# Second state sum moved ahead of the first gate product, and three weight requests reordered

## The chip, the cores and the metric

The kernel runs on one NeuronCore of a Trainium2 chip. The metric is the device time of one execution in microseconds (us); less is better. The engines named below are PE (TensorE, matrix products), DVE (VectorE), ACT (ScalarE), POOL (GpSimd) and SP (SyncE, which here only issues transfers). ACT issues transfers too.

## The reference

Two blocks follow one another, all in float32. First an mLSTM cell over batch 4, 8 heads, 768 steps, head size 40: for each step t it computes

```
m_new = max(f + m, i)
C = exp(f + m - m_new) * C + exp(i - m_new) * outer(v, k)
n = exp(f + m - m_new) * n + exp(i - m_new) * k
y = sigmoid(o) * (C q) / max(|n.q|, 1)
```

Then y is put together to 3072 tokens by 320 features, x, and a gated feed-forward block computes `(silu(x @ w_gate) * (x @ w_val)) @ w_out`, with 1536 hidden features.

The arrays reach the kernel in their own number format. The three weight matrices are 64-bit floats there: one weight is two 32-bit words, and the kernel makes a float32 of them.

## The kernel before, in words

**Tiles and groups.** The 768 steps are cut into six groups of 128 steps. The 32 heads of the batch are handled in two halves, called pairs P = 0 and P = 1, of 16 heads each. For a group the cell is computed with matrix products: scores inside the group, products with the state carried in, and an addition to the state. The result, x transposed (`xT`), is 320 features by 512 tokens (four batches of 128 steps).

**Feed-forward.** The 1536 hidden features are twelve chunks m of 128. `hidden(g, m)` (L643) does ten matrix instructions, which the trace records as 20 products of 512 columns (L648): they fill two PSUM banks, one for the gate and one for the value. ACT takes the Silu of the first (L653) and DVE multiplies it with the second into `h_sb` (L654). There are four banks of the kind "gen", so chunk m + 2 can begin only once ACT and DVE have read chunk m. `project` and `project_all` then multiply by `w_out`.

**The order of work.** Every engine's order is written out by hand: it is the order of the calls in the text. In group 0's feed-forward, lists named `ahead` and `slots` say what is done beside chunk m. In particular `slots[5]` and `slots[6]` hold the transposes of the next group's k and q, `slots[6]` and `slots[7]` the decay weights of the next group (`weights_sub` on DVE, L451, then `weights_mask` on POOL, L456), `slots[8]` their exponentials on ACT.

**Weights.** They come in pieces (`PIECES`, L138): pieces 0 and 1 hold one chunk each, pieces 2 to 6 two chunks each (piece 2: chunks 2 and 3, and so on), pieces 7 to 9 hold `w_out`. `piece_load` (L140) asks for a piece in two halves: the gate half goes to partitions 0 to 63, the value half to partitions 64 to 127. A half of pieces 2 to 6 is 640 KB. SP asks for the gate half. ACT asks for the value half of pieces 0 to 4, SP for those of pieces 5 and 6. A request waits in its engine's order like any other instruction, and the requests of one engine form one transfer queue.

A loaded chunk is made float32 by `convert`: `scale` (two passes on ACT, L190 and L192), `join` (two on DVE, L199 and L200) and `rounded` (L207, an addition on POOL, or on DVE where it is told so). Only then can PE multiply with it. Chunks 2 to 11 are converted inside the chunks before.

**The stretch around the change.** It is the end of the first group's cell, at 22 to 43 us. `sig` (L463) are the two sigmoids of the output gate on ACT. `first_own` and `first_x` make x, `first_gate` multiplies it with the sigmoid on DVE, `first_seam` transposes it to `xT`. Between the two seams stand six constant products, `burn(6, "gen")` (L469), on data that nothing reads. `first_state(P, eng)` (L547) sums the first group's state over its 128 steps with 16 matrix instructions for one pair (32 recorded, L552) and lets `eng` copy the sum to the state. `first_state(0, A)` runs before chunk 0, `first_state(1, A)` after it, in `slots[0]`. `slots[0]` also asks for the next group's k and q, which overwrite what the state sums read. The state is first needed by the next group, at 85 us.

SP's requests behind the weights are, in order: `M_sb` to `M_dram` (L611), k and q of the next group (L117), piece 6 (L165), `w_sb` from `M_dram` (L447, the next group's maxima), v, and so on.

Of the kernel before, what the change touches and what calls it, by code (L numbers as in the profile page):

```python
# [12 lines left out]
U32 = mybir.dt.uint32  # L13
# [11 lines left out]
def kernel(  # L25
# [18 lines left out]
    nc = tc.nc  # L44
# [7 lines left out]
    D1 = D + 1  # L52
# [4 lines left out]
    NKC = DM // HP  # L57
    UH = BH // 2
    UA = UH // 2
    NH = NFC + 1  # L60
# [15 lines left out]
    def bank(name, tag="cell"):  # L76
        return psum.tile([128, 512], F32, name=name, tag=tag)

    def half(i):
        return slice(i * SUB, (i + 1) * SUB)  # L80
# [5 lines left out]
    def heads(P):  # L86
        return slice(P * UH, (P + 1) * UH)

    k_sb = const.tile([128, BH, DP], F32)
    q_sb = const.tile([128, BH, DP], F32)  # L90
# [10 lines left out]
    wo_sb = const.tile([128, NFC, DM], F32)  # L101
    h_sb = const.tile([128, NH, TW], F32)
# [16 lines left out]
    def copy(eng, dst, src):  # L119
        if eng is nc.scalar:  # L120
            nc.scalar.copy(dst, src)
        else:
            eng.tensor_copy(dst, src)
# [13 lines left out]
    raws = {}  # L137
    PIECES = [("gv", 0, 1), ("gv", 1, 1)] + [("gv", m, 2) for m in range(2, NFC, 2)] + [("o", m, 4) for m in range(0, NFC, 4)]  # L138

    def piece_load(p, home=None):  # L140
        kind, m, n = PIECES[p]
        if kind == "gv":
            a, d = NKC, n * 128
            src = [(slice(i * HP, (i + 1) * HP), w[:, m * 128:(m + n) * 128].rearrange("(c p) f -> p c f", p=HP))
                   for i, w in enumerate((moe_w_gate, moe_w_val))]
            queues = (nc.sync, nc.scalar if p < 5 else nc.sync)
        else:
            a, d = n, DM
            src = [(slice(0, 128), moe_w_out[m * 128:(m + n) * 128].rearrange("(a p) d -> p a d", p=128))]
            queues = (nc.sync,)  # L150
        if src[0][1].dtype == F32:
            for r, w in src:
                if kind == "o":
                    nc.sync.dma_start(out=wo_sb[r, m:m + n, :], in_=w)
                else:
                    for x in range(n):
                        nc.sync.dma_start(out=wgv_sb[r, m + x], in_=w[:, :, ts(x, 128)])
            return
        if home is None:
            raw = conv.tile([128, 4 * NKC * 128], U32, name="raw")  # L160
        else:
            raw = home.rearrange("p a t -> p (a t)").bitcast(U32)
        raw = raw[:, 0:2 * a * d]
        for (r, w), queue in zip(src, queues):
            queue.dma_start(out=raw[r].rearrange("p (a d) -> p a d", a=a), in_=w.bitcast(U32))  # L165
        words = raw.rearrange("p (a d two) -> p a d two", two=2, a=a)
        raws[p] = (words[:, :, :, 0], words[:, :, :, 1])
        split(p)
# [4 lines left out]
    def split(p):  # L173
        if p in raws:
            lo, hi = raws.pop(p)
            kind, m, n = PIECES[p]
            if kind == "gv":
                for c in range(n):
                    r = slice(c * 128, (c + 1) * 128)
                    blocks[m + c] = (lo[:, :, r], hi[:, :, r], wgv_sb[:, m + c])  # L180
            else:
                for c in range(0, n, 2):
                    blocks[NFC + (m + c) // 2] = (lo[:, c:c + 2], hi[:, c:c + 2], wo_sb[:, m + c:m + c + 2, :])

    def scale(j):
        if j in blocks:
            lo, hi, dst = blocks[j]
            a, d = hi.shape[1], hi.shape[2]
            top = conv.tile([128, NKC * 128], F32, name="top", bufs=1).rearrange("p (a d) -> p a d", a=a)
            nc.scalar.mul(top, hi.bitcast(F32), 2.0 ** -112)  # L190
            low = conv.tile([128, NKC * 128], I32, name="low").rearrange("p (a d) -> p a d", a=a)
            nc.scalar.mul(low, lo, 2.0 ** -29)  # L192
            blocks[j] = (low, top.bitcast(U32), dst)

    def join(j):
        if j in blocks:
            lo, top, dst = blocks[j]
            both = dst.bitcast(U32)
            nc.vector.tensor_scalar(both, top, scalar1=3, scalar2=None, op0=ALU.logical_shift_left)  # L199
            nc.vector.scalar_tensor_tensor(both, in0=top, scalar=0x80000000, in1=both, op0=ALU.bitwise_and,  # L200
                                           op1=ALU.bitwise_or)
            blocks[j] = (lo, dst.bitcast(I32))

    def rounded(j, eng=None):
        if j in blocks:
            lo, dst = blocks.pop(j)
            (eng or nc.gpsimd).tensor_tensor(dst, dst, lo, op=ALU.add)  # L207

    def convert(j, eng=None):
        scale(j)  # L210
        join(j)
        rounded(j, eng)
# [34 lines left out]
    for u in range(B):  # L247
        r = slice(u * BH, (u + 1) * BH)
# [92 lines left out]
        eng.tensor_tensor(vw_sb[:, heads(P)], v_sb[:, heads(P)], w_sb[:, heads(P), last].to_broadcast([128, UH, D1]),  # L341
                          op=ALU.mult)

    def small(name, n=UA):
        return bank(name)[:, 0:n * D1].rearrange("p (a d) -> p a d", d=D1)

    def add(n, P):
        ps = [small("add") for _ in range(2)]
# [8 lines left out]
    def state(s):  # L357
        return C_ring[s % 3]
# [103 lines left out]
    def sig(P):  # L462
        nc.scalar.activation(o_sb[:, heads(P)], o_sb[:, heads(P)], AF.Sigmoid)  # L463


    def burn(n, tag="cell"):
        t = bank("burn", tag)
        for _ in range(n):
            nc.tensor.matmul(t, lhsT=junk[:, 0:128], rhs=junk, start=True, stop=True)  # L469
# [4 lines left out]
    A, V, G = nc.scalar, nc.vector, nc.gpsimd  # L474
# [66 lines left out]
    def first_gate(P):  # L541
        for u in (2 * P, 2 * P + 1):
            x = x_sb[:, u, 0:DM].rearrange("p (h d) -> p h d", d=D)
            nc.vector.tensor_tensor(x, x, o_sb[:, u * H:(u + 1) * H], op=ALU.mult)
        nc.gpsimd.tensor_copy(x_sb[:, 2 * P:2 * P + 2, DM:], x_sb[:, 2 * P:2 * P + 2, 0:HP])

    def first_state(P, eng):  # L547
        ps = small("add")
        for a in range(UA):
            for two in range(2):  # L550
                h = P * UH + 2 * a + two
                nc.tensor.matmul(ps[half(two), a, :], lhsT=k_sb[:, h, :], rhs=vw_sb[:, h, :], start=True, stop=True)  # L552
        copy(eng, state(2)[:, P * UA:(P + 1) * UA], ps)

    def first_seam(P, engs):
# [23 lines left out]
    first_turn(1, q_sb, qT, (A, V))  # L579
    load(o_sb, o_gate, 0, 1)  # L580
    piece_load(0)
    piece_load(1)
    late_maxima()
    first_own(1)
    first_values(1)
    first_scores(1)
    first_x(1)
    sig(0)
    sig(1)
    piece_load(2, h_sb[:, NH - NKC:])  # L590
    piece_load(3, wo_sb)
    burn(3)
    first_own(2)
    first_own(3)
# [3 lines left out]
    first_seam(0, (A, A, V))  # L598
    scale(0)
    first_gate(1)  # L600
    burn(6, "gen")
    piece_load(4)
    join(0)
    first_seam(1, (A, A, V))
    rounded(0, V)
    first_state(0, A)
    late_decay()
    convert(1)
    nc.scalar.activation(step1, step1, AF.Exp)
    piece_load(5)  # L610
    nc.sync.dma_start(out=M_dram, in_=flat(M_sb))  # L611
# [105 lines left out]
    def load_all(dst, a, n):  # L717
# [3 lines left out]
    run = lambda f, *a: (lambda: f(*a))  # L721
# [3 lines left out]
    ahead = {m: [m + 2] for m in range(4)}  # L725
    ahead.update({4: [6], 5: [7, 8], 6: [9], 7: [10], 8: [11], 9: [], 10: [], 11: []})
    slots = {
        0: [run(first_state, 1, A), run(load_all, k_sb, k, 1), run(load_all, q_sb, q, 1)],
        1: [run(piece_load, 6, h_sb[:, NH - NKC:]), run(decay_rows)],
        2: [run(late_turns), run(weights_load, 1), run(load_all, v_sb, v, 1)],  # L730
        3: [run(decay)],
# [45 lines left out]
    for g in range(1, NG):  # L777
        n, f = g + 1, g + 2
# [67 lines left out]
```

## Time and profile before

| | us |
|---|---|
| median of 3 runs | 555.15 (554.77 to 555.56) |
| the profiled execution, its own time | 555.16 |
| its span in the profile | 553.0 |
| PE busy in the span | 546.4 (99%) |
| DVE busy | 234.4 (42%) |
| ACT busy | 134.7 (24%) |
| POOL busy | 106.6 (19%) |

A line of a timeline gives start and duration in us, the engine, the line of the code, the operation and its tiles, and how often; what stands in brackets is the engine's idle time before it and what ended it. PEld is PE's loading of weights. ACTq and SPq are requests for transfers, which take no time of the engine's arithmetic. The chain of work is followed back from the last instruction: at each step to what released it. Waits are put down to the releaser that came last. The DMA share is that of the core's 16 transfer engines.

### The profile page before, as it was taken

To read this page: it belongs to the slowest core of one execution; us is meant where nothing else is said; L and a number is where in the kernel's file an instruction comes from. 1 tells how busy PE (TensorE), PEld (TensorE's weight loads), DVE (VectorE), ACT (ScalarE), POOL (GpSimd) and SP (SyncE) were. 2 spreads that over 40 slices of the span, in tenths; PEclk is the share of its full clock that TensorE was granted. 3 is DMA by queue.
4 is the path that set the end of the run, shared out by engine and by line. 5 is a ranking of instruction groups with operands and counts; after the bars stand their busy time and mean duration, and the time that the engine had idled before them with its cause. 6 is when DMAs were issued, how large, how long until landed. Compare 5 with 4: busy or idle time off the path is not lost.

```text
span 553.0 us, 11595 instructions
## 1 busy us (share of the span) xinstructions
PE 546.4 (99%) x4992; PEld 312.9 (57%) x4992; DVE 234.4 (42%) x394; ACT 134.7 (24%) x202; POOL 106.6 (19%) x97
## 2 busy tenths in 40 slices
PE   8999999999999999999999999999999999999997
PEld 4955546675545575544576455466455567444475
DVE  5956687962156332445521445531426621011100
ACT  4366564443101033110124101005110100111100
POOL 2314355574011151011133001114001200000000
PEclk9999999999999999999999999999999999999999
DMA  9999996798631763660464451395000131000000
GB/s 125 177 280 187 192 274 115 155 111 125 68 49 17 108 109 83 71 76 5 82 127 104 53 68 27 49 149 107 13 1 2 29 62 43 12 1 0 2 24 24
DMA packets 223994, 45.69 MB, mean 83 GB/s; under 512 B 214504, under 2 KB 219112, under 8 KB 223944
## 3 DMA queue, kind: packets, MB, share of 16 engines
q1 hardware_dynamic: 222036, 42.11, 46.7%
q10 hardware_dynamic: 1908, 2.85, 2.0%
q8 instruction: 39, 0.64, 0.5%
q14 instruction: 11, 0.09, 0.1%
HBM read 35.68 MB, written 4.01 MB: 72 GB/s over the span
## 4 chain that ended last, share of the span: by engine, by line
PE 92%; DMA 4%; SPq 3%; POOL 0%; DVE 0%; ACT 0%; issue 0%; ACTq 0%; POOLq 0%
PE gv_ps L648 55%; PE o_ps L664 24%; PE o_ps L671 5%; SPq L117 3%; DMA h_sb<-in_moe_w_val_dram 2%; PE inter L377 2%; PE sp L331 2%; PE intra L382 2%; DMA o_sb<-in_o_gate_dram 2%; PE add L353 1%; PE tp_kq L296 0%; POOL wgv_sb L207 0%; PE tp_x L439 0%; DVE wgv_sb L200 0%; ACT top L190 0%
## 5 line engine op out<-in xcount | busy, mean ns | idle before, releaser
L648 PE MATMUL gv_ps<-xT,wgv_sb 64*128 64x512 f32 x1440 | 317.3, 593 | 1.6 <-POOL wgv_sb L207 1.1
L648 PEld LDWEIGHTS gv_ps<-xT,wgv_sb 64*128 64x128 f32 x1440 | 139.1, 187 | 159.4 <-issue 154.6
L654 DVE TENSOR_TENSOR h_sb<-sg,gv_ps 128x512 f32<-128x512 f32 x72 | 49.5, 687 | 214.5 <-ACT sg L653 214.4
L664 PE MATMUL o_ps<-wo_sb,h_sb 128*128 128x320 f32 x480 | 130.5, 433 | 0.0
L664 PEld LDWEIGHTS o_ps<-wo_sb,h_sb 128*128 128x128 f32 x480 | 90.8, 190 | 41.0 <-issue 3.8
L653 ACT ACTIVATE sg<-gv_ps 128x512 f32<-128x512 f32 x72 | 43.0, 597 | 268.6 <-PE gv_ps L648 268.5
L362 POOL TENSOR_TENSOR C<-C,dec 128x328 f32<-128x328 f32 x20 | 14.5, 735 | 137.7 <-DVE C L369 137.6
L456 POOL TENSOR_SCALAR_AFFINE_SELECT w_sb<-w_sb 64x1024 f32<-64x1024 f32 x20 | 27.8, 1388 | 60.2 <-DVE w_sb L451 59.3
L658 ACT COPY z_sb<-o_ps 128x320 f32<-128x320 f32 x24 | 10.0, 422 | 94.7 <-PE o_ps L664 90.9
L403 POOL TENSOR_TENSOR o_sb<-o_sb,y_sb 128x640 f32<-128x640 f32 x10 | 14.3, 1428 | 79.2 <-DVE y_sb L394 79.1
L671 PE MATMUL o_ps<-wo_sb,h_sb 128*128 128x320 f32 x96 | 26.9, 437 | 0.0
L451 DVE TENSOR_TENSOR w_sb<-g_T,w_sb 128x1024 f32<-128x1024 f32 x10 | 13.2, 1355 | 27.6 <-DMA w_sb<-M_dram 27.6
L426 DVE STREAM_TRANSPOSE xT<-x_sq 128x640 f32<-128x640 f32 x16 | 12.5, 822 | 23.7 <-DMA x_sq<-x_sb 23.7
L671 PEld LDWEIGHTS o_ps<-wo_sb,h_sb 128*128 128x128 f32 x96 | 17.9, 190 | 7.2
L394 DVE TENSOR_TENSOR y_sb<-y_sb,intra 64x328 f32<-64x328 f32 x40 | 19.7, 493 | 0.8 <-PE intra L382 0.2
L369 DVE TENSOR_TENSOR C<-C,add 40x328 f32<-40x328 f32 (+1 forms) x36 | 17.7, 493 | 1.3 <-PE add L353 0.4
L207 POOL TENSOR_TENSOR wgv_sb<-wgv_sb,low 128x640 int32<-128x640 int32 x8 | 12.3, 1541 | 23.7 <-DVE wgv_sb L200 21.9
L377 PEld LDWEIGHTS inter<-C,qT 64*64 64x64 f32 x640 | 10.2, 134 | 7.3 <-issue 6.1
L341 POOL TENSOR_TENSOR vw_sb<-v_sb,w_sb 128x656 f32<-128x656 f32 x10 | 12.8, 1303 | 0.4
L338 DVE TENSOR_TENSOR w_sb<-sp,w_sb 128x512 f32<-128x512 f32 x20 | 12.7, 682 | 0.0
L460 ACT ACTIVATE w_sb<-w_sb 128x1024 f32<-128x1024 f32 x10 | 10.6, 1058 | 8.8 <-POOL w_sb L456 8.8
L397 DVE TENSOR_SCALAR den<-den 128x16 f32<-128x16 f32 x10 | 12.2, 1216 | 0.3
(129 smaller groups left out, 343.7 us busy)
## 6 DMA issues: line engine op xcount, KB each, us to landing
w_sb<-M_dram SPq DMA_DIRECT2D x10, 512.0 KB, 7.2
x_sq<-x_sb SPq DMA_DIRECT2D x128, 40.0 KB, 2.0
k_sb<-in_k_dram SPq DMA_DIRECT2D x12, 320.0 KB, 6.1
v_sb<-in_v_dram SPq DMA_DIRECT2D x12, 320.0 KB, 5.7
o_sb<-in_o_gate_dram SPq DMA_DIRECT2D x12, 320.0 KB, 5.4
raw<-in_moe_w_out_dram SPq DMA_DIRECT2D x3, 1280.0 KB, 7.8
out_dram<-z_sb SPq DMA_DIRECT2D x24, 160.0 KB, 1.8
q_sb<-in_q_dram SPq DMA_DIRECT2D x32, 64.0 KB, 2.4
```

Of the source, the lines that this page charges most:

```text
L117: nc.sync.dma_start(out=dst[:, heads(P), 0:D], in_=tokens(a, c, P))
L362: nc.gpsimd.tensor_tensor(state(s + 1)[:, a], state(s)[:, a], dec[:, s - 2, a].unsqueeze(2).to_broadcast([128, UA, D1]), op=ALU.mult)
L369: nc.vector.tensor_tensor(c, c, ps[r], op=ALU.add)
L377: nc.tensor.matmul(inter[two][half(i), a, :], lhsT=qT[half(two), P * UA + a, half(i)], rhs=state(2 * n + i)[half(two), P * UA + a, :], sta ...
L394: nc.vector.tensor_tensor(t, t, intra[i][half(c)], op=ALU.add)
L403: eng.tensor_tensor(o, o, y[:, :, 0:D], op=ALU.mult)
L456: nc.gpsimd.affine_select(w, w, compare_op=ALU.is_ge, fill=NEG, base=0, pattern=[[0, UH], [1, SUB]], channel_multiplier=-1)
L648: nc.tensor.matmul(ps[i], lhsT=wgv_sb[half(i), m, PAIRS[kc][i] if g < 2 else kc, :], rhs=x[half(i), kc, :], start=(kc == 0), stop=(kc == N ...
L653: nc.scalar.activation(sg, ps[0], AF.Silu)
L654: nc.vector.tensor_tensor(hid(g, m), sg, ps[1], op=ALU.mult)
L664: nc.tensor.matmul(p, lhsT=hid(g, m)[:, ts(u, L)], rhs=wo_sb[:, m, :], start=(m == 0), stop=(m == NFC - 1))
L671: nc.tensor.matmul(ps[u], lhsT=hid(g, m)[:, ts(u, L)], rhs=wo_sb[:, m, :], start=(m == 0), stop=(m == NFC - 1))
```

## The change

It has three parts.

1. The state sum of pair 1 is taken between the two seams, into a PSUM bank of the kind "gen". One constant product stays there instead of six. The copy of the sum to the state is split off (`first_kept`) and done by DVE, after the copy of pair 0's sum by ACT; `slots[0]` no longer has it.
2. `convert(1)` gets DVE for its last addition, instead of POOL.
3. Requests for three value halves move. Piece 2's two halves are asked for after the first sigmoid instead of after the second. Piece 3's gate half is asked for with them, but its value half waits (`later=True`) until `value_half(3)`, behind `convert(1)`. Piece 4's value half is asked for by SP instead of ACT.

```diff
+    asks = {}
+
+    def value_half(p):
+        for ask in asks.pop(p, ()):
+            ask()
+
-    def piece_load(p, home=None):
+    def piece_load(p, home=None, later=False):
...
-            queues = (nc.sync, nc.scalar if p < 5 else nc.sync)
+            queues = (nc.sync, nc.scalar if p < 4 else nc.sync)
...
-        for (r, w), queue in zip(src, queues):
-            queue.dma_start(out=raw[r].rearrange("p (a d) -> p a d", a=a), in_=w.bitcast(U32))
+        asks[p] = [lambda r=r, w=w, queue=queue: queue.dma_start(out=raw[r].rearrange("p (a d) -> p a d", a=a), in_=w.bitcast(U32))
+                   for (r, w), queue in zip(src, queues)]
+        asks[p].pop(0)()
+        if not later:
+            value_half(p)
...
-    def small(name, n=UA):
-        return bank(name)[:, 0:n * D1].rearrange("p (a d) -> p a d", d=D1)
+    def small(name, n=UA, tag="cell"):
+        return bank(name, tag)[:, 0:n * D1].rearrange("p (a d) -> p a d", d=D1)
...
-    def first_state(P, eng):
-        ps = small("add")
+    def first_state(P, tag="cell"):
+        ps = small("add", tag=tag)
...
+        return ps
+
+    def first_kept(P, ps, eng):
         copy(eng, state(2)[:, P * UA:(P + 1) * UA], ps)
...
     sig(0)
+    piece_load(2, h_sb[:, NH - NKC:])
+    piece_load(3, wo_sb, later=True)
     sig(1)
-    piece_load(2, h_sb[:, NH - NKC:])
-    piece_load(3, wo_sb)
...
-    burn(6, "gen")
+    ps1 = first_state(1, "gen")
+    burn(1, "gen")
     piece_load(4)
...
-    first_state(0, A)
+    first_kept(0, first_state(0), A)
+    first_kept(1, ps1, V)
     late_decay()
-    convert(1)
+    convert(1, V)
+    value_half(3)
...
-        0: [run(first_state, 1, A), run(load_all, k_sb, k, 1), run(load_all, q_sb, q, 1)],
+        0: [run(load_all, k_sb, k, 1), run(load_all, q_sb, q, 1)],
```

## The prediction

> **What bounds the kernel now.** I read the page's engine shares and its chain first, then the timelines of PE, ACT and DVE where the diff acts, then DMA throughput by window.
>
> ```profile
> PE 546.4 (99%) x4992; PEld 312.9 (57%) x4992; DVE 234.4 (42%) x394; ACT 134.7 (24%) x202; POOL 106.6 (19%) x97
> ...
> PE 92%; DMA 4%; SPq 3%; POOL 0%; DVE 0%; ACT 0%; issue 0%; ACTq 0%; POOLq 0%
> ```
>
> TensorE is the bound: 92% of the chain. A saving counts if it shortens PE's stream and nothing later hands the time back. PE's timeline, start and duration first:
>
> ```profile
> 30.24 1.13 PE L552 MATMUL add<-vw_sb,k_sb 128*64 128x41 f32 x32
> 31.90 4.56 PE L648 MATMUL gv_ps<-xT,wgv_sb 64*128 64x512 f32 x20 [0.53 <-DVE m_in L285]
> 36.39 1.13 PE L552 MATMUL add<-vw_sb,k_sb 128*64 128x41 f32 x32
> 37.45 4.56 PE L648 MATMUL gv_ps<-xT,wgv_sb 64*128 64x512 f32 x20
> 43.10 4.80 PE L648 MATMUL gv_ps<-xT,wgv_sb 64*128 64x512 f32 x20 [1.08 <-POOL wgv_sb L207]
> ```
>
> Gate products of chunks 0, 1 and 2 start at 31.90, 37.45 and 43.10. Between 0 and 1 stand the second pair's state sums (36.39 to 37.45, 1.06 us); before 2 PE idles 1.08 us for the converted weights. ACT's timeline says why:
>
> ```profile
> 25.43 0.60 ACTq L165 DMA_DIRECT2D h_sb<-in_moe_w_val_dram  x1
> 39.17 0.80 ACT L190 ACTIVATE top<-h_sb 128x640 f32<-128x640 f32 x1 [3.66 <-DMA h_sb<-in_moe_w_val_dram]
> ```
>
> The value half of piece 2, asked for at 25.43, lands 13.6 us later, at 39.0. From there scaling, joining and rounding take 4.1 us to 43.10.
>
> After that PE has no gap until 100 us, but other engines run close. The timeline of 68 to 83 us:
>
> ```profile
> 68.54 13.10 PE L648 MATMUL gv_ps<-xT,wgv_sb 64*128 64x512 f32 x60
> 70.97 1.22 DVE L451 TENSOR_TENSOR w_sb<-g_T,w_sb 128x1024 f32<-128x1024 f32 x1 [1.31 <-DMA w_sb<-M_dram]
> ...
> 72.64 1.64 DVE L200 SCALAR_TENSOR_TENSOR wgv_sb<-top,wgv_sb 128x640 uint32<-128x640 uint32 x1
> ...
> 74.41 1.54 DVE L207 CUSTOM_DVE_ANT_0 wgv_sb<-wgv_sb,low 128x1280 uint16<-128x1280 uint16 x1
> 75.87 0.68 DVE L654 TENSOR_TENSOR h_sb<-sg,gv_ps 128x512 f32<-128x512 f32 x1
> ```
>
> The 60 products are chunks 7, 8, 9. DVE waits for the transfer w_sb until 70.97, then works without a pause; the product of chunk 7 (75.87) ends at 76.55. It frees the PSUM pair that chunk 9 uses, and chunk 9 starts at 68.70 + 2 x 4.31 = 77.3 (chain of work). So chunk 9 stands only 0.75 us behind a chain that starts at a DMA landing and not at PE.
>
> What sets that landing is SP's transfer queue. The windows (PE, PEld, DVE, ACT, POOL busy, clock, DMA share, GB/s):
>
> ```profile
> 28.00:32.00 4.00, 3.46 (x49) 2.45 (x48) 3.62 (x10) 2.93 (x7) 0.29 (x1) 1.00 1.06 194
> 37.00:43.00 6.00, 5.02 (x38) 2.25 (x34) 1.72 (x3) 3.79 (x6) 1.49 (x1) 1.00 1.05 353
> 44.00:47.00 3.00, 3.00 (x17) 2.60 (x15) 2.93 (x8) 2.24 (x4) 1.55 (x1) 1.00 1.07 201
> 58.00:63.00 5.00, 5.00 (x48) 2.60 (x46) 3.27 (x5) 4.03 (x7) 1.55 (x1) 1.00 1.07 205
> ```
>
> While only SP's requests run (28 to 32, 44 to 47, 58 to 63) some 200 GB/s move; while ACT's run beside them (37 to 43), 353. In all four the engines are full. I read it as: moving a half from ACT's queue to SP's lengthens SP's line.
>
> [...]
>
> **The change, part by part.**
> 1. Second state sum ahead. 1.06 us of products leave the stretch between chunks 0 and 1. They take the place of five constant products (six took 1.46 us, so 1.2 us) while PE waits for DVE's gated x (PEld waits until 28.68 and 29.08). The inputs are long there (POOL's weighted values end 22.44). Cost 0; without that cover 1.06. Its sum sits in a bank of the four that chunk 0 and 1 use, the one that chunk 1 takes first; DVE's copy frees it at 32.2 (next part), chunk 1 wants it at 36.39. Gain: 1.06.
> 2. The copy of that sum moves from ACT (0.43 at 42.46) to DVE (some 0.45), and the rounding of chunk 1 from POOL (1.53, ending 35.84) to DVE (0.82). DVE's line becomes: rounded 0 to 31.76, copy to 32.2, decay to 33.2, join to 34.6, rounding to 35.4; chunk 1 wants it at 36.39. DVE idles 5.84 us behind that, which hides both. Without that cover 1.3 us.
> 3. Value half of piece 2: ACT issues it between the two sigmoids, at 22.35 instead of 25.43. With the same 13.6 us it lands at 36.0; with the shorter line ahead (it passes the gate halves of pieces 2 and 3, asked for at 22.94 and 23.69), nearer 34. Chunk 2 now wants to start at 31.90 + 2 x 4.49 = 40.9, so a landing by 36.8 is enough. Gain: 43.10 - 40.9 = 2.2 us in all, the 1.06 of part 1 included. Alone, part 1 would gain nothing: chunk 2 would still start at 43.10.
> 4. Value half of piece 3: from 26.07 to behind chunk 1's scaling on ACT, some 33.6. Behind its issue (0.6 us) wait the exponential and piece 2's scaling; ACT idles 3.66 there, so 0. It must land by 47.2 (chunk 4 wanted at 53.52 - 2.2 = 51.3, less 4.1). With 10 to 13.6 us it lands at 43.6 to 47.2.
> 5. Value half of piece 4: from ACT's queue (30.04) to SP's (30.9). SP's line before w_sb is now one half longer. 640 KB (655,360 bytes) at 200 GB/s is 3.3 us. Part comes back, since one half fewer shares with ACT: SP's halves landed at 33.3, 37.7, 41.5, 46.0 and 50.2, four in 16.9 us or 4.2 each instead of 3.3, 3.6 us lost to three of ACT's, 1.2 each; by throughput only 0.45 (half of 353 against 200, over 3.7 us). So w_sb is later by 2.1 to 2.9; I take 2.5. Lower bound 0 or somewhat less: near 49 to 50 the trace moved only 33 GB/s, a hole of some 1.5 us that the extra half may fill. Queued behind it on SP: M, second k, q, piece 6, w_sb, v. The first q landed at 56.5 and the second at 60.3; 2.5 later they come at 59.0 and 62.8, and their transposes (62.70 and 68.04) want them 2.2 earlier, at 60.5 and 65.8: no wait.
>
> Sum at chunk 9: PE could start it at 77.3 - 2.2 = 75.1. DVE's chain gives 76.55 + 2.5 = 79.05. So chunk 9 starts near 79.1, 1.8 us later than before, after some 4 us of idle PE. Behind it (exponentials 79.28, weighted values to 85.28 against use at 88.08, product of chunk 8 to 82.04 against 83.59) everything hangs on w_sb or on PE and moves along; the rest of the kernel is PE-bound and keeps the difference. The profiled execution took 555.16 (span 553.0), the median is 555.15: 555.16 + 1.75 = 556.9.
>
> **Rivals.** A change within 0.2%, about 1.1 us, is what a measurement of this kernel can't tell from none.
> - *The gain stays (faster).* One mechanism: w_sb isn't later, because the hole at 49 to 50 us and the earlier half of piece 2 make up for the extra half. Then chunk 9 starts at 76.6: 554.4. It decides from w_sb landing before 70.6; at 69.4 or sooner the whole 2.2 us stays, 553.0. For it: the hole. Against: the hole was there although requests were queued[...].
> - *Half of each (same).* The hole takes 1.5 of the 2.5: w_sb 1.0 later, chunk 9 at 77.6: 555.4.
> - *Piece 3 is late (slower).* If its value half takes 18.1 us, as piece 4's did from ACT, it lands at 51.7 and chunk 4 starts at 55.8 instead of 53.52: 557.5. Against: those 18 us were spent behind two other ACT halves, which are now gone.
> - *The half of piece 2 isn't sooner.* Then chunk 2 stays at 43.10; chunk 9 still waits for DVE: 556.9 again.
>
> **How the numbers follow.** w_sb late 0.52 (with the unmoved piece 2 in it), piece 3 late 0.10, half of each 0.21, gain stays 0.17. So faster 0.17, same 0.21, slower 0.62. Predicted 556.9; its own range 556.2 to 557.8 (w_sb 1.8 to 3.4 later). The whole range: low 553.4, which holds the 554.4 and leaves out the full gain; high 558.6[...].
>
> **What would show it.** Right: chunk 2 near 40.9 without a wait; PE idle of 3 to 4 us before chunk 9, released by DVE L669; DVE waiting for w_sb to about 73.5; SP's piece-5 halves landing 2 to 3 us later. Wrong: w_sb landed by 71; a PE gap before chunk 4; chunk 0 much later than 31.9.

## The result, and the profile after

The changed kernel takes 559.0 us (median of 14 executions, 557.34 to 562.69), the kernel before on the same chip 555.28 us (14 executions, 554.14 to 557.62). The ratio is 1.0066, 95% interval 1.0044 to 1.0089: 3.7 us slower. The prediction was 556.9 us, range 553.4 to 558.6; the sign was right, the size was not.

The profiled execution took 561.73 us with a span of 559.5; it is one of four above 561.5, so its trace shows more than the median's loss, and the experiments below bring the usual case.

The page of the changed kernel, busy time and chain of work:

```profile
PE 547.4 (98%) x4987; PEld 317.5 (57%) x4987; DVE 234.4 (42%) x396; ACT 134.2 (24%) x201; POOL 104.5 (19%) x96
...
PE 93%; SPq 3%; DMA 3%; DVE 0%; issue 0%; ACT 0%; ACTq 0%
...
L663 PE MATMUL gv_ps<-xT,wgv_sb 64*128 64x512 f32 x1440 | 319.6, 597 | 5.5 <-DVE wgv_sb L216 5.5
```

PE's work has not grown in count (4987 against 4992 instructions). What is new is in the last line: the gate products waited 5.5 us for a converted weight chunk, and 5.5 of 5.5 is one wait. ACT's timeline says which transfer that was:

```profile
22.50 0.60 ACTq L170 DMA_DIRECT2D h_sb<-in_moe_w_val_dram  x1
28.08 0.74 ACT L472 ACTIVATE o_sb<-o_sb 128x640 f32<-128x640 f32 x1 [4.84 <-DMA o_sb<-in_o_gate_dram]
34.26 0.77 ACT L199 ACTIVATE top<-raw 128x640 f32<-128x640 f32 x1 [4.48 <-DMA raw<-in_moe_w_gate_dram]
36.55 0.60 ACTq L170 DMA_DIRECT2D wo_sb<-in_moe_w_val_dram  x1
```

The value half of piece 2 is asked for at 22.50 (before: 25.43). The second output gate then arrives only at 28.08 (before: 25.42), and the gate half of piece 0, which SP had asked for at 19.56, at 34.26 instead of 28.50. The table of DMA queues for the stretches of 24 to 26 and 26 to 28 us says what ran in between (packets, MB, share of the 16 transfer engines):

```profile
q10 hardware_dynamic: 250, 0.35, 104.0%
q1 hardware_dynamic: 77, 0.01, 10.1%
...
q10 hardware_dynamic: 193, 0.36, 100.2%
q1 hardware_dynamic: 10, 0.01, 2.6%
```

q10 is ACT's queue and q1 is SP's: over the whole execution the change took 336 packets and 0.65 MB from q10 (1908 to 1572 packets) and gave them to q1, which is piece 4's half. So for 4 us ACT's queue had the engines to itself, while SP's, with the output gate and the gate halves of pieces 0 and 1 asked for earlier, moved almost nothing. Chunk 0 is late for that reason. PE's timeline, where the gap stands in brackets:

```profile
37.62 15.26 PE L663 MATMUL gv_ps<-xT,wgv_sb 64*128 64x512 f32 x60 [5.54 <-DVE wgv_sb L216]
```

Chunks 0, 1 and 2 do follow each other without a wait, as predicted, but from 37.62 and not from 31.90. They take 15.26 us, where the same 60 products take 13.15 in other runs: the windows of 32 to 37 and 37 to 43 us (busy time by engine, then the clock, the DMA share and GB/s) show a lowered clock at the end of the gap and behind it:

```profile
32.00:37.00 5.00, 0.09 (x4) 0.00 (x0) 1.91 (x4) 2.74 (x6) 0.00 (x0) 0.81 1.06 196
37.00:43.00 6.00, 5.38 (x16) 2.58 (x18) 5.22 (x10) 5.95 (x7) 0.40 (x1) 0.59 1.07 205
```

The last number is telling too: 205 GB/s from 37 to 43 us, where the kernel before moved 353. The moved ACT requests no longer run beside SP's: from 32 to 42 us only q1 moved data, although piece 3's value half was asked for at 36.55. SP's timeline:

```profile
35.73 0.60 SPq L170 DMA_DIRECT2D raw<-in_moe_w_gate_dram  x1
36.37 0.61 SPq L170 DMA_DIRECT2D raw<-in_moe_w_val_dram  x1
...
43.76 12.82 SPq L117 DMA_DIRECT2D k_sb<-in_k_dram  x2
...
63.36 8.60 SPq L456 DMA_DIRECT2D w_sb<-M_dram  x2
```

Piece 4 goes into the buffer of piece 0, so SP asks for it only when ACT has scaled chunk 0: 1.5 us behind the scaling's start, at 35.73 (before: 30.26). All that SP asks for afterwards moves along, and w_sb, before at 56.61, is asked for at 63.36. DVE's timeline:

```profile
77.14 1.23 DVE L460 TENSOR_TENSOR w_sb<-g_T,w_sb 128x1024 f32<-128x1024 f32 x1 [2.50 <-DMA w_sb<-M_dram]
...
82.04 0.67 DVE L669 TENSOR_TENSOR h_sb<-sg,gv_ps 128x512 f32<-128x512 f32 x1
```

In the kernel before these two stood at 70.97 and 75.87. The product at 82.04 frees the bank pair of chunk 9. In this execution chunk 9 waited only 0.4 us for it, because PE was already late by itself.

Of the 6.5 us between the two profiles (559.5 against 553.0), 5.7 are there when chunk 9 is done: the next products on PE start at 87.25 instead of 81.56. The other 0.8 us is a pause on PE further on (1.16 us instead of 0.33), to which the last section comes back.

### The profile page after: what moved, and what is told of

Read it like the earlier page. It is cut to its first block, busy times and chain, and to the rows that moved or that the text cites. A ratio compares the mean times of both kernels' runs of the same rounds, so it can differ in the third digit from the quotient of the medians.

```text
span 559.5 us, 11586 instructions
## 1 busy us (share of the span) xinstructions
PE 547.4 (98%) x4987; PEld 317.5 (57%) x4987; DVE 234.4 (42%) x396; ACT 134.2 (24%) x201; POOL 104.5 (19%) x96
## 3 DMA queue, kind: packets, MB, share of 16 engines
q10 hardware_dynamic: 1572, 2.20, 2.0%
## 4 chain that ended last, share of the span: by engine, by line
PE 93%; SPq 3%; DMA 3%; DVE 0%; issue 0%; ACT 0%; ACTq 0%
PE gv_ps L663 57%; PE o_ps L679 23%; PE o_ps L686 5%; SPq L117 3%; DMA raw<-in_moe_w_gate_dram 3%; PE inter L386 2%; PE sp L340 2%; PE intra L391 2%; PE add L362 1%; PE tp_kq L305 0%; PE tp_x L448 0%; DVE wgv_sb L209 0%; DVE wgv_sb L216 0%; ACT top L199 0%; SPq L132 0%
## 5 line engine op out<-in xcount | busy, mean ns | idle before, releaser
L663 PEld LDWEIGHTS gv_ps<-xT,wgv_sb 64*128 64x128 f32 x1440 | 144.3, 188 | 161.2 <-issue 150.4
L216 POOL TENSOR_TENSOR wgv_sb<-wgv_sb,low 128x640 int32<-128x640 int32 x7 | 10.8, 1538 | 29.5 <-DVE wgv_sb L209 29.5
L199 ACT ACTIVATE top<-raw 128x640 f32<-128x640 f32 x12 | 9.6, 798 | 12.8 <-issue 6.1
```

Of the source, the lines that this page charges most:

```text
L663: nc.tensor.matmul(ps[i], lhsT=wgv_sb[half(i), m, PAIRS[kc][i] if g < 2 else kc, :], rhs=x[half(i), kc, :], start=(kc == 0), stop=(kc == N ...
```

## The experiments

Five theories appear in the expectations. **E**: the early request of piece 2's value half delays piece 0's gate half, and so chunk 0, in all executions. **R**: it does so in some executions only, by the order in which queued transfers happen to go. **L**: the extra half in SP's queue makes w_sb, and so chunk 9, late. **C**: a gap on PE is paid twice, by its length and by a stretch of lowered clock behind it (in the first profile of piece 4 on SP: a gap of 1.49 us, then 3.42 us at half clock, and 18 products in 6.25 us instead of 4.56). **W**: the waits alone make up the loss. "Changed" and "before" are the two kernels of the case; times are medians.

### One part at a time

The sums ahead and their copy and rounding on DVE, no request moved:

```diff
-            queues = (nc.sync, nc.scalar if p < 4 else nc.sync)
+            queues = (nc.sync, nc.scalar if p < 5 else nc.sync)
...
-    piece_load(2, h_sb[:, NH - NKC:])
-    piece_load(3, wo_sb, later=True)
     sig(1)
+    piece_load(2, h_sb[:, NH - NKC:])
+    piece_load(3, wo_sb)
...
-    value_half(3)
```

> Parts 1 and 2 of the change alone (state sum ahead, its copy and chunk 1's addition on DVE); every request where it was before. Theory E (piece 2's value half, asked for early, goes ahead of piece 0's gate half and makes chunk 0 late) and theory L (the extra half in SP's queue makes w_sb late): both leave this kernel as it was. Chunk 2 still waits for a landing near 39.0 and starts near 43.1, so the 1.06 us that leave PE's stream turn into a longer wait there (some 2.2 instead of 1.1 us). Time within 0.3 us of before. Only a theory that blames the copies on DVE would see it slower by 1 us or more, with chunk 0 or 1 late.

Measured: 555.27 us over 22 executions, ratio 1.0008 (0.9997 to 1.0018). Chunks 0 and 1 stand together, and PE waits ahead of chunk 2 instead:

```profile
32.20 8.85 PE L662 MATMUL gv_ps<-xT,wgv_sb 64*128 64x512 f32 x40 [0.28 <-DVE wgv_sb L216]
42.20 4.80 PE L662 MATMUL gv_ps<-xT,wgv_sb 64*128 64x512 f32 x20 [1.15 <-POOL wgv_sb L216]
```

So parts 1 and 2 are free and gain nothing by themselves, as predicted. In the profiled execution (556.46 us, one of the slower ones) the wait is 1.15 us and not 2.2, and chunk 2 starts 0.9 us sooner than in the kernel before; the pause further on, 2.25 us here, takes that back.

The kernel before with piece 2 asked for between the two sigmoids:

```diff
     sig(0)
-    sig(1)
     piece_load(2, h_sb[:, NH - NKC:])
+    sig(1)
```

> The kernel before with one edit: piece 2 is asked for between the two sigmoids (ACT's value half some 3 us sooner). E: piece 0's gate half lands at 32 to 34 us instead of 28.4, chunk 0 starts 3.5 to 5.7 us late, the time is 2.5 to 5 us longer. L: SP's line holds what it held, w_sb lands near 71, chunk 2 has no wait, time 554.4 to 555.2.

Measured: 554.91 us over 22 executions, ratio 1.0014 (0.9997 to 1.0032), but with a wider spread than before: 13 from 553.1 to 555.0, 8 from 556.4 to 559.2, one at 561.21.

The kernel before with piece 4's value half on SP's queue:

```diff
-            queues = (nc.sync, nc.scalar if p < 5 else nc.sync)
+            queues = (nc.sync, nc.scalar if p < 4 else nc.sync)
```

> The kernel before with one edit: piece 4's value half is asked for by SP. L: SP's halves of piece 5 and w_sb land 2.1 to 2.9 us later (w_sb near 73.5 instead of 70.97), chunk 9 starts 1.8 us late, 556.9. E: the early part is as before (chunk 0 at 31.9); if the line doesn't matter by itself, w_sb stays near 71 and the time within 0.3 us of before.

Measured: 557.31 us over 11 executions, ratio 1.0043 (1.0026 to 1.0060). DVE's and PE's timelines of this kernel:

```profile
73.80 1.23 DVE L451 TENSOR_TENSOR w_sb<-g_T,w_sb 128x1024 f32<-128x1024 f32 x1 [4.39 <-DMA w_sb<-M_dram]
```

```profile
79.42 6.25 PE L648 MATMUL gv_ps<-xT,wgv_sb 64*128 64x512 f32 x18 [1.49 <-DVE h_sb L654]
```

w_sb is 2.83 us later than before (70.97), and chunk 9's wait ends 2.1 us later than the 77.3 of before. Theory L holds: this one edit costs some 2.3 us. PE's line also shows 18 products in 6.25 us instead of 4.56; that is taken up below.

### The changed kernel with one part undone

Piece 2 and the gate half of piece 3 asked for after both sigmoids again:

```diff
     sig(0)
-    piece_load(2, h_sb[:, NH - NKC:])
-    piece_load(3, wo_sb, later=True)
     sig(1)
+    piece_load(2, h_sb[:, NH - NKC:])
+    piece_load(3, wo_sb, later=True)
```

> The changed kernel with piece 2 (and the gate half of piece 3) asked for after both sigmoids, as before; the rest of the change stays. E: chunk 0 is back at 31.9, piece 0's gate half lands near 28.4; all of the loss that came from the early request is gone. With L besides: chunk 2 at 41 to 43.1, w_sb near 73.5, chunk 9 late by 1.8, 556.9. E without L: 555.3 or, if chunk 2 is sooner, 554.4.

Measured: 558.07 us over 6 executions (557.32 to 559.26), ratio 1.0059 (1.0039 to 1.0078). Undoing the early request brings the typical time down by 1 us at most, and no execution is above 559.3. It was repeated later, below.

The changed kernel once more, for a second profile:

> The changed kernel once more, for a second profile and for its spread beside the kernel before on the same chip. Theory L+R (the extra half in SP's queue costs some 2.5 us at w_sb in every execution; besides, a race: where piece 2's value half gets ahead of the second output-gate transfer and of piece 0's gate half, those land 3 and 6 us late and chunk 0 starts near 37.6): most executions near 3.2 us above before with chunk 0 at 32 to 34 and w_sb near 74, a minority 6 to 7 us above. Theory E alone (the early request costs 5.7 us at chunk 0 in all executions): chunk 0 at 37.6 again and no second group.

Measured: 559.68 us over 10 executions, ratio 1.0090 (1.0055 to 1.0124): six from 556.75 to 560.23, four from 562.63 to 564.08. The profiled one took 563.49. ACT's timeline again has the late gate half of piece 0, less late than in the first profile:

```profile
31.38 0.79 ACT L199 ACTIVATE top<-raw 128x640 f32<-128x640 f32 x1 [1.98 <-DMA raw<-in_moe_w_gate_dram]
```

w_sb is subtracted at 77.60, and chunk 9 follows a gap of 4.34 us.

Piece 4's value half back on ACT's queue:

```diff
-            queues = (nc.sync, nc.scalar if p < 4 else nc.sync)
+            queues = (nc.sync, nc.scalar if p < 5 else nc.sync)
```

> The changed kernel with one edit undone: piece 4's value half is asked for by ACT again. L+R: SP's line is as long as before, w_sb lands 2.5 us sooner than in the changed kernel, between 70.5 and 72; the time falls by 2 to 3 us to within 1 us of before, with some executions 3 to 6 us above where the race goes the other way. E: no gain, 558 to 562 as in the changed kernel.

Measured: 558.17 us over 22 executions, ratio 1.0052 (1.0036 to 1.0069), where more was expected back. A new wait came in. PE and ACT of this kernel:

```profile
53.83 8.85 PE L663 MATMUL gv_ps<-xT,wgv_sb 64*128 64x512 f32 x40 [1.16 <-POOL wgv_sb L216]
```

```profile
49.91 0.79 ACT L199 ACTIVATE top<-wo_sb 128x640 f32<-128x640 f32 x1 [6.63 <-DMA raw<-in_moe_w_val_dram]
```

ACT asks for piece 4's half at 30.86 and for piece 3's only at 33.74, so piece 3 stands behind piece 4 in ACT's queue, lands at 49.9, and chunk 4 waits 1.16 us. In the changed kernel the later request of piece 3 needs piece 4 to be out of ACT's queue; the two edits belong together.

w_sb asked for ahead of piece 6:

```diff
-        1: [run(piece_load, 6, h_sb[:, NH - NKC:]), run(decay_rows)],
-        2: [run(late_turns), run(weights_load, 1), run(load_all, v_sb, v, 1)],
+        1: [run(weights_load, 1), run(piece_load, 6, h_sb[:, NH - NKC:]), run(decay_rows)],
+        2: [run(late_turns), run(load_all, v_sb, v, 1)],
```

> The changed kernel with one edit: SP asks for w_sb ahead of piece 6 instead of behind it (two halves of 3.3 us each). L+R: w_sb lands 4 to 7 us sooner (67 to 70), DVE no longer waits there, chunk 9 isn't held by it; but piece 6 lands some 5 us later, and the scaling of chunk 10 on ACT, which stands ahead of the Silu of chunk 7, may take that place. Time 1 to 2.2 us below the changed kernel, 556 to 558. A theory in which w_sb isn't on the path: no change against the changed kernel.

Measured: 558.62 us over 22 executions (554.41 to 562.80), ratio 1.0058 (1.0036 to 1.0080). w_sb was subtracted at 70.51, sooner than in the kernel before, and yet PE waits longer:

```profile
79.09 1.12 PE L663 MATMUL gv_ps<-xT,wgv_sb 64*128 64x512 f32 x2 [1.79 <-ACT sg L668]
80.87 3.78 PE L663 MATMUL gv_ps<-xT,wgv_sb 64*128 64x512 f32 x8 [0.66 <-DVE h_sb L669]
```

Now piece 6 comes last. SP's whole line is late, and whoever stands at its end pays.

w_sb asked for ahead of the next group's q instead, so that piece 6 keeps its place:

```diff
-        0: [run(load_all, k_sb, k, 1), run(load_all, q_sb, q, 1)],
+        0: [run(load_all, k_sb, k, 1), run(weights_load, 1), run(load_all, q_sb, q, 1)],
...
-        2: [run(late_turns), run(weights_load, 1), run(load_all, v_sb, v, 1)],
+        2: [run(late_turns), run(load_all, v_sb, v, 1)],
```

> The changed kernel with the transfer of w_sb asked for ahead of the two loads of q, instead of behind q, piece 6: piece 6 keeps its time, q comes some 2.6 us later and has more than that to spare. Theory L with C (late w_sb and the lost clock behind it make up 3.7 of the loss): DVE no longer waits for w_sb, chunk 9 follows chunk 8 without a gap, the lower executions come to 553.5 to 555.5, those in which piece 0's gate half is late to 557 to 559, the median to 554.5 to 556. If the loss sat elsewhere (piece 3 late, the order of the early transfers alone): 557.5 to 559.

Measured: 561.89 us over 15 executions, ratio 1.0098 (1.0072 to 1.0124). A miss: I had given q room that it doesn't have. PE's timeline:

```profile
69.17 1.11 PE L305 MATMUL tp_kq<-ident,q_sb 64*128 64x64 f32 x16 [3.83 <-DMA q_sb<-in_q_dram]
```

Together the last two say that the lateness is one of SP's line as a whole, which neither of these two orders removes.

### Is it the clock?

Eleven constant products between chunks 8 and 9 of the changed kernel:

```diff
-            run(piece_load, 8)],
+            run(piece_load, 8), run(burn, 11)],
```

> The changed kernel with eleven constant products (about 0.25 us each, 2.75 us) issued on TensorE between chunk 8 and chunk 9, where it otherwise idles for the pair that DVE frees; nothing else is touched, so the transfers stay as late as they were. Theory C (an idle stretch on TensorE is paid twice, by its length and by about 3.4 us at half clock behind it, 1.7 us): the product that frees chunk 9's pair stays where it is, the clock behind the gap stays 1.00, and the median falls from about 559.0 to 557.2 to 557.8; executions with a mean clock of 1.000, of which the changed kernel had none in 24, appear. Theory W (waits alone make up the loss): 558.8 to 559.5, or more, since the fill is not free where the gap is shorter than 2.75 us.

Measured: 559.82 us over 22 executions, ratio 1.0079 (1.0057 to 1.0100): eleven from 556.82 to 558.83, eleven from 560.81 to 564.63. The lower half fits theory C, the median does not, and with half of the executions in the upper group the run decides nothing.

So the clock was tried where that group does not occur: piece 4's half on SP's queue and nothing else, without and with five constant products in the gap.

```diff
-            run(piece_load, 8)],
+            run(piece_load, 8), run(burn, 5)],
```

> The kernel before with piece 4's value half on SP's queue and nothing else, again, as the partner of the next run. Both theories: 556.8 to 557.8; a gap of about 1.5 us ahead of chunk 9.

> The same with five constant products (1.25 us) between chunks 8 and 9, so that the gap of 1.5 us is nearly filled and the lateness of w_sb unchanged. Theory C: no lowered clock behind the gap, 18 products of chunk 9 in 4.56 us and not 6.25, median 0.8 to 1.7 us under the partner's. Theory W: within 0.4 us of the partner.

Measured: 557.26 us without (6 executions, ratio 1.0051, 1.0031 to 1.0071) and 557.25 with (6 executions, ratio 1.0056, 1.0038 to 1.0074). PE's timeline with the fill:

```profile
75.95 1.25 PE L469 MATMUL burn<-junk 128*128 128x512 bf16 x4
77.13 5.25 PE L648 MATMUL gv_ps<-xT,wgv_sb 64*128 64x512 f32 x20
```

The gap is closed, the clock stays at 1.00, and the time is the same. In this execution, and in the profiled one without the fill (gap 1.06 us, clock 1.00), the clock was never low there; in the first run of this edit it was. Six executions against six leave room for a difference of 1 us and more either way. The mean clocks of the 17 executions of this edit without the fill are clearer: nine have 0.999 or 1.000, and their median is 557.47; the other eight, with 0.994 to 0.997, have 557.21. So executions that lost nothing to the clock are as slow as the rest. For piece 4's half on SP's queue this speaks for theory W: a lowered clock behind the gap ahead of chunk 9 is real in single executions, but it is not what the median lost.

For the changed kernel itself the question is not settled: all of its 24 executions have a mean clock of 0.997 or less, so each had at least one lowered stretch.

### The requests of pieces 2 and 3

The sums ahead and piece 4's half on SP, with pieces 2 and 3 as before; against the kernel with the sums alone:

```diff
-            queues = (nc.sync, nc.scalar if p < 5 else nc.sync)
+            queues = (nc.sync, nc.scalar if p < 4 else nc.sync)
```

> The sums ahead (parts 1 and 2) with piece 4's value half on SP, pieces 2 and 3 as before the change: the changed kernel without both moved requests. If the later request of piece 3 costs something[...], this is 0.8 to 1.5 us faster than piece 2 back (558.75 over 17 executions): 557.3 to 558.0. If it costs nothing: 558.3 to 559.0.

> The changed kernel with pieces 2 and 3 as before the change, again, as the partner of the next two: 556.5 to 557.3, w_sb subtracted on DVE from 72.2 to 72.8.

Measured: 556.86 us (7 executions, ratio 1.0050, 1.0031 to 1.0070) and 556.97 us (12 executions, ratio 1.0039, 1.0026 to 1.0053).

To it, the later request of piece 3 is added (the changed kernel with piece 2 back, the edit shown above):

> The changed kernel with piece 2 (and the gate half of piece 3) asked for after both sigmoids again, as in the run before of the same edit, now with enough executions to see whether the upper group (561.5 to 564, 8 of 24 in the changed kernel) is still there. Theory R (the early request of piece 2's value half gets ahead of the second output gate and of piece 0's gate half, in some executions, and makes that group): no execution above 560.5, or at most one, median 557.8 to 558.5. If the group has another cause: a third of the executions at 561.5 or more.

> The same and piece 3's value half asked for behind chunk 1's scaling (the changed kernel with piece 2 back). If the later request lengthens SP's line: 1.0 to 1.9 us over the partner, w_sb from 73.6 to 74.0. If the difference was one of chips and of chance: within 0.5 us of the partner.

Measured: 558.85 us (11 executions, ratio 1.0064, 1.0042 to 1.0087; one of them above 560.5) and 559.23 us (5 executions, ratio 1.0068, 1.0056 to 1.0080). On one chip (the second of each pair) that is 2.3 us more than without, and the two intervals don't meet. DVE's line for w_sb in the profiled executions of that pair, first without the later request, then with it:

```profile
73.98 1.23 DVE L460 TENSOR_TENSOR w_sb<-g_T,w_sb 128x1024 f32<-128x1024 f32 x1 [4.33 <-DMA w_sb<-M_dram]
```

```profile
74.16 1.22 DVE L460 TENSOR_TENSOR w_sb<-g_T,w_sb 128x1024 f32<-128x1024 f32 x1 [4.14 <-DMA w_sb<-M_dram]
```

They are 0.18 us apart, but the first execution (558.51 us) was among the slowest of its kernel, and the one of the run before had w_sb at 72.50. With the later request the three profiles have 73.60, 73.91 and 74.16, without it (with or without the sums) 72.20, 72.50, 72.56, 73.80 and 73.98. The time of the profiled execution follows this number in all eight: 556.46 to 557.12 us with w_sb by 72.56, and 558.51 to 559.03 with w_sb at 73.60 or later. So the loss is where theory L looks for it, ahead of chunk 9. Why w_sb is late in all three profiles with the later request, and in only two of the five without it, the traces don't show. The piece itself came in time: in the profile of piece 2 back it landed at 46.75, within the 47.2 of the prediction, and chunk 4 did not wait.

To the same partner, the earlier request of piece 2 alone is added (the changed kernel with piece 3 not later):

```diff
-    piece_load(3, wo_sb, later=True)
+    piece_load(3, wo_sb)
...
-    value_half(3)
```

> The partner and piece 2's value half asked for between the two sigmoids (the changed kernel with piece 3 not later). Theory R: most executions at the partner's 556.5 to 558, but a quarter to a half of them 3 to 5 us higher. If the upper group needs piece 3's later request too: no execution above 560.

Measured: 559.51 us over 8 executions (556.09 to 561.74), ratio 1.0068 (1.0044 to 1.0091): three from 556.1 to 557.3, three from 559.3 to 559.9, two at 561.0 and 561.7. The median is 2.5 us above the partner's on the same chip, but the two intervals (the partner's is 1.0026 to 1.0053) meet. The profiled one took 557.29 and shows the change as it was meant, on ACT and PE:

```profile
28.41 0.81 ACT L199 ACTIVATE top<-raw 128x640 f32<-128x640 f32 x1
```

```profile
32.16 13.15 PE L662 MATMUL gv_ps<-xT,wgv_sb 64*128 64x512 f32 x60 [0.28 <-DVE wgv_sb L216]
...
78.75 4.56 PE L662 MATMUL gv_ps<-xT,wgv_sb 64*128 64x512 f32 x18 [3.15 <-DVE h_sb L668]
```

Piece 0 is in time, chunks 0 to 2 run through from 32.16, PE gains its 2.2 us and loses them in a gap of 3.15 us ahead of chunk 9.

So theory E, a loss in all executions, falls. Theory R is best seen across the profiles. Nine profiled executions asked early for piece 2's value half on ACT's queue; in five of them the first scaling on ACT waited 1.91 to 4.48 us for piece 0's gate half (it began at 30.65 to 34.26 us), in four it did not wait. In the eleven that asked later, or on SP's queue, the longest such wait was 0.69 us. The queues agree: in the five, SP's queue moved at most 0.01 MB from 24 to 26 us and at most 0.06 MB from 26 to 28, and ACT's 0.33 to 0.41 MB in each; in the four, SP's moved 0.12 to 0.30 and 0.28 to 0.35 MB. And of executions above 560.5 us, the changed kernel had 8 of 24, with piece 2 back 1 of 22, and the kernel before none of 215.

### Two tries at a faster kernel

First: the sums ahead, piece 2's value half on SP's queue behind its gate half, w_sb ahead of piece 6, and the conversions of chunks 10 and 11 one chunk later. In this kernel chunk 8's product on DVE (79.19) overwrites words of piece 6 before ACT scales those of chunk 11 (81.18), so chunk 11 is computed with other weights; the instructions are those of the same work.

```diff
-            queues = (nc.sync, nc.scalar if p < 4 else nc.sync)
+            queues = (nc.sync, nc.scalar if p in (0, 1, 3, 4) else nc.sync)
...
-    ahead.update({4: [6], 5: [7, 8], 6: [9], 7: [10], 8: [11], 9: [], 10: [], 11: []})
+    ahead.update({4: [6], 5: [7, 8], 6: [9], 7: [], 8: [10], 9: [11], 10: [], 11: []})
...
-        1: [run(piece_load, 6, h_sb[:, NH - NKC:]), run(decay_rows)],
-        2: [run(late_turns), run(weights_load, 1), run(load_all, v_sb, v, 1)],
+        1: [run(weights_load, 1), run(piece_load, 6, h_sb[:, NH - NKC:]), run(decay_rows)],
+        2: [run(late_turns), run(load_all, v_sb, v, 1)],
```

> Parts 1 and 2 of the change with other requests: piece 2's value half is asked for by SP behind its gate half, those of pieces 3 and 4 by ACT after the second sigmoid, w_sb ahead of piece 6, and the conversions of chunks 10 and 11 each one chunk later. L: chunk 2 no longer waits (landing near 36.7, start near 41), w_sb lands by 70 in spite of the extra half, chunk 9 isn't held; 553.0 to 554.0, 1 to 2 us below before. If piece 6, now last, holds chunk 10 or 11 instead: 554 to 556.

Measured: 556.06 us over 22 executions, ratio 1.0027 (1.0009 to 1.0044).

Second: the sums ahead, piece 2 between the sigmoids, w_sb ahead of q, pieces 3 and 4 as before. Against the kernel with the sums alone:

```diff
-    sig(1)
     piece_load(2, h_sb[:, NH - NKC:])
+    sig(1)
     piece_load(3, wo_sb)
...
-        0: [run(load_all, k_sb, k, 1), run(load_all, q_sb, q, 1)],
+        0: [run(load_all, k_sb, k, 1), run(weights_load, 1), run(load_all, q_sb, q, 1)],
...
-        2: [run(late_turns), run(weights_load, 1), run(load_all, v_sb, v, 1)],
+        2: [run(late_turns), run(load_all, v_sb, v, 1)],
```

> A try at a version faster than both: the second pair's sum ahead and its copy and rounding on DVE, piece 2 asked for between the two sigmoids, the value halves of pieces 3 and 4 where they were before the change, and w_sb asked for ahead of the loads of q. Theory L with C: chunk 2 at 40.9 to 42, no wait for w_sb, chunk 9 near 75.5, so 553.0 to 554.0 where piece 0's gate half lands in time, and 556 to 558 in the executions where it doesn't. If something else holds chunk 9 or a later chunk: 554.5 to 555.5, no better than before.

Measured: 556.92 us over 22 executions (553.58 to 560.30), ratio 1.0023 (1.0005 to 1.0041). In the profiled one piece 0's gate half came at 31.30, chunk 0 at 34.70. Neither beats the kernel before.

## Why the prediction was right and wrong

Two steps failed, both on requests for transfers (parts as the prediction numbers them): part 4, which put the later request of piece 3 at 0, and part 3, which put the early request of piece 2 down as a gain without a cost. What each part costs, from medians (before: 554.8 to 555.3 in its sets):

| kernel | executions | median us | over 560.5 |
|---|---|---|---|
| sums ahead, DVE (parts 1 and 2) | 22 | 555.27 | 0 |
| piece 4's half on SP alone | 17 | 557.31 | 0 |
| both | 19 | 556.86 | 0 |
| both, piece 3 later | 22 | 558.76 | 1 |
| both, piece 2 early | 8 | 559.51 | 2 |
| both, piece 3 later, piece 2 early: the changed kernel | 24 | 559.13 | 8 |

The parts don't add up: on one chip, over the partner's 556.97, piece 3 later costs 2.3 us and piece 2 early 2.5, and the changed kernel, with both, is at 559.13 (on other chips), no slower than with one. So a price of its own can't be given to either within the changed kernel.

**Parts 1 and 2** (sums and DVE, nothing by themselves): right, 555.27 against 554.95 on that chip, with the wait ahead of chunk 2 where it was said to be, if shorter (1.15 us instead of some 2.2).

**Part 5** (piece 4's half on SP's queue; w_sb 2.1 to 2.9 later, taken as 2.5; chunk 9 near 79.1; 556.9 in all): right in mechanism, and near enough in size. w_sb moved by 1.2 to 3.0 us in the five profiles without the other requests (by 2.83 and 1.59 with that edit alone, where chunk 9's wait ended at 79.42 and 78.19). The sum of 556.9 us is what the sums and piece 4's half make without the other requests: 556.86 and 556.97. The prediction's own rival said so: without the early piece 2 it is 556.9 again, since chunk 9 waits for DVE.

**Part 4** (piece 3's half later, "so 0"): wrong, and the step that is missing from the sum at the median. Its landing was well estimated and chunk 4 didn't wait, but the kernel with it is 1.9 us slower over all executions (558.76 against 556.86), 2.3 us on one chip. I had asked only when the piece must be there, and not what SP's and ACT's transfers lose when its traffic moves into another stretch. The size is shown, and the profiles place the loss ahead of chunk 9, where w_sb comes later; what in the transfers makes it later is not shown.

**Part 3** (piece 2's half early, a gain of 2.2 us in all): wrong too, and behind most of the slowest executions. It said that the request passes the gate halves of pieces 2 and 3. But SP's queue still held the second output gate and the gate halves of pieces 0 and 1 at 22 us, and the same request gets ahead of these too, in five of the nine profiled executions. Then chunk 0 comes at 34.0 to 37.6 us, SP cannot ask for piece 4 before chunk 0 is scaled, and the whole of SP's line follows. "Chunk 0 much later than 31.9" stood among the signs of a wrong prediction and had no price; it is what the first profile shows (37.62). The landing had been taken as a fixed 13.6 us behind the request; in that profile it was 9.8, and from 24 to 28 us the half ran almost alone (0.71 MB on ACT's queue, 0.02 on SP's). The trace of before already held a sign that the two queues don't simply share: from 26 to 32 us SP's queue moved 0.39 MB in every 2 us and ACT's nothing, although the halves of pieces 2 and 3 had been asked for at 25.43 and 26.07. Where the race is won, the gain of 2.2 us is there and is lost ahead of chunk 9, as predicted (3.15 us of idle PE where about 4 were expected).

**The high end** (558.6, an estimate of mine that the trace of before doesn't show): half clock behind an idle PE did happen, in some executions, and after gaps as short as 1.49 us. With piece 4's half alone it is not in the median. In the changed kernel's slow executions it is: 15.26 us instead of 13.15 for chunks 0 to 2 in the first profile, 6.91 instead of 4.56 for the 18 products behind the gap of 4.34 us in the second. What it adds to the changed kernel's median is open. The 558.6 was too low mainly for want of parts 3 and 4, which cost 1.9 us and more without any place in the sum.

Of the rivals, "gain stays" fell with w_sb, "piece 3 late" was right that piece 3 costs and wrong on how, since its chunk did not wait. "Half of each" fell as well: where w_sb kept its place in SP's order, it was later by 1.2 us or more in every profile with piece 4's half on SP, and no kernel with that half there had a median under 556.8. Left open: why the later request of piece 3 makes w_sb late, what decides which queue runs first, and how much of the changed kernel's median is lowered clock.

## What to carry to other kernels

A request moved ahead in one engine's order can get ahead of what is still queued on the other engine, not only of what stands behind it in the text (here it did in five of nine profiled executions, and piece 0's first scaling waited 1.91 to 4.48 us): list what is under way at that moment and ask which of it is needed first. Look for the transfer whose buffer's release gates the next request: here its lateness moved a whole queue along (w_sb was asked for at 63.36 us instead of 56.61). And "it lands in time" doesn't make a move free: price the queue that it leaves and the one that it joins, and look at several executions, since one profile can show either outcome of a race. A rate per queue and stretch, beside the total rate, tells which of two queues is moving (here 0.35 MB against 0.01 in 2 us).

## What the runs showed of the hardware

**The clock.** TensorE's clock went down to 0.50 for 3.42 us in each of three profiles whose windows hold a whole such stretch: piece 4 on SP and piece 2 back, again (both from 80 to 84 us), and the second try (26 to 30 us). In the changed kernel's first profile it stood at 0.50 for 6.83 us, twice as long: windows of 0.1 us have it from 35.09 to 41.91, so it began inside the gap of 5.54 us that ended at 37.62. A gap was not needed. In the kernel before with piece 2 early, windows of 24 to 27 and 27 to 31 us:

```profile
24.00:27.00 3.00, 3.00 (x29) 3.00 (x29) 2.83 (x11) 0.00 (x0) 0.29 (x1) 1.00 1.15 205
27.00:31.00 4.00, 4.00 (x19) 2.73 (x18) 3.12 (x11) 2.54 (x4) 0.44 (x1) 0.57 1.07 289
```

The stretch behind the first group's small products (32 products of 41 columns in 3.66 us, with PE counted as busy) ran at half speed, and chunk 0 came at 33.75 instead of 31.90. In eight other profiles the same stretch was at half speed (0.50 from 28 to 29 us), in that of the kernel before it was not (1.00 from 27 to 31). By the lengths above, one such stretch makes the mean clock of an execution 0.997 (half of 3.42 us in 553), and the first profile of piece 4 on SP has that figure; 73 of 201 executions of the kernel before had 0.996 or 0.997. Their medians were only 0.2 to 0.6 us higher in each set, which fits that chunk 2 waits for a transfer anyway.

Gaps ahead of chunk 9 of 1.49 us (piece 4 on SP) and 1.62 us (piece 2 back, again) were followed by half clock, which made 18 products take 6.25 us instead of 4.56; gaps of 1.06, 1.23, 1.43, 2.40 and 3.15 us were not. The windows for 81 to 83 us, of the kernel with piece 4 on SP and of the kernel before:

```profile
81.00:83.00 2.00, 2.00 (x8) 0.70 (x6) 1.86 (x2) 0.50 (x1) 1.95 (x2) 0.50 1.02 395
```

```profile
81.00:83.00 2.00, 2.00 (x100) 1.44 (x100) 1.03 (x2) 1.98 (x2) 1.92 (x2) 1.00 1.08 174
```

So half clock followed a gap of 1.49 us and did not follow one of 3.15: the length of a gap did not decide it. What did is not shown.

**Landings that differ between executions.** In the changed kernel, piece 0's gate half let the first scaling begin at 34.26 in one profile and at 31.38 in the other; with piece 2 early and piece 3 not later, at 28.41. That the order of transfers on two queues can differ so from one execution to the next I had not expected. Nor did the two queues share in one way: in the kernel before, each moved 0.33 to 0.37 MB in every 2 us from 38 to 44 us, but from 26 to 32 us SP's moved 0.39 and ACT's nothing; in the changed kernel, ACT's moved 0.35 and 0.36 MB and SP's 0.01 each from 24 to 28 us. Both times the queue that stood still, or nearly so, had requests outstanding. Why a queue stands still, and for which of the two, no run here shows.

**A pause at one place of PE's instructions.** In 14 of the 20 profiles PE pauses among the `intra` products of the next group, at some 101 to 108 us, for 0.16 to 2.25 us, and the trace shows nothing that ends it. The changed kernel, the same with eleven constant products more, and piece 4's half on SP with five more:

```profile
107.51 0.60 PE L391 MATMUL intra<-v_sb,w_sb 64*64 64x41 f32 x25 [1.16 <-issue]
```

```profile
104.16 0.78 PE L391 MATMUL intra<-v_sb,w_sb 64*64 64x41 f32 x36 [0.16 <-issue]
```

```profile
102.67 0.78 PE L382 MATMUL intra<-v_sb,w_sb 64*64 64x41 f32 x35 [1.39 <-issue]
```

Eleven products more ahead of it leave eleven more behind it (36 against 25), and five more leave five more (35 against the 30 of the kernel before). So the pause belongs to a place in the stream of instructions and not to these products or their data. What PE waits for there is not shown.
